# Spacing the attention groups 104 columns apart instead of 99, in the queries and keys, the scores and the masked weights

## The chip, the cores and the metric

The kernel runs on one core of one Trainium2 chip. The metric is device time in microseconds (us), the median over the executions of a run; times of a kernel on one chip scatter by about 0.3 to 1.6 us around 1248. Engines are named as in the profile: PE is the matmul engine (PEld its weight loads), DVE the vector engine, ACT the scalar engine, POOL the GpSimd engine, SP the engine that issues most loads and stores.

## The reference, cut to what matters

The reference computes two unrelated parts from two inputs of 2048 rows and joins them. Part A is a complex linear recurrence with a projection before and after it. Part B, which the change touches, is an attention over segments of 32 rows with 8 memory rows carried along:

```python
for s in range(n_seg):                       # 64 segments
    h = jnp.concatenate([mem, xs], axis=1)   # 8 memory rows + 32 rows
    q, k, v = (einsum('btd,dhe->bhte', h, W) for W in (Wq, Wk, Wv))   # 32 heads of 128
    scores = einsum('bhqe,bhke->bhqk', q, k) * scale
    p = softmax(where(mask, scores, -1e9))
    o = einsum('bhte,hed->btd', einsum('bhqk,bhke->bhqe', p, v), Wo)
    mem = o[:, :M, :]; outs.append(o[:, M:, :])
```

The kernel gathers three segments and three memory columns into a group of 99 columns; 22 groups for each head cover the input.

## The kernel before

Queries and keys of two heads (a "pair", 16 of them) lie in one tile each, group after group, 99 columns (198 bytes in bf16) apart. A score group is two groups of two heads: four score matmuls, one exponential on ACT, one product with the mask on POOL. The value matmuls take the masked product `m` as their weights. `psS` holds scores, `psO` and `psR` the values, `psP` projections.

```python
NG = 22; GX = 96; GW = 99; NU = NG // 2
QW = 2208
MW = 4 * GW + 29
...
    def att_front(self, hp, u):              # one score group
        qt, kt = self.qk[hp % 2]
        s = k.ps("S", (128, 2, 2, GW))
        for gg in range(2):
            g0 = (2 * u + gg) * GW
            for hh in range(2):
                PE.matmul(s[:, gg, hh, :], kt[:, hh, g0:g0 + 128], qt[:, hh, g0:g0 + GW], start=True, stop=True)
        e = self.p3a.tile([GW, 2, 2, GW], BF16, name="b_e", bufs=3)
        k.S.activation(e[:], s[0:GW], ACT.Exp, ...)
        m = self.mt[i % len(self.mt)]
        k.G.tensor_tensor(m[0:GW, 0:4 * GW].rearrange(...), e[:], mask..., ALU.mult)
...
    def att_back(self, blocks):              # up to three blocks of values
        for i, (_, b, m, j) in enumerate(blocks):
            PE.matmul(o[:, i, 0:EV], m[:, j * GW:j * GW + 128], vt[...], start=True, stop=True)
...
    def attention(self):
        for hp in range(HP):
            for u in range(NU):
                if u == 2:
                    self.load_v(hp + 1)
                pend += self.att_front(hp, u)
                back(8)                      # value matmuls in threes until 8 blocks are left
                yield hp, u                  # projections of the next pair fill in here
        back(0)
```

The evictions of projections into `q` and `k` are DVE copies of 480 columns, cut into five runs of 96 at the group spacing.

Of the kernel before, what the change touches and what calls it, by code (L numbers as in the profile page):

```python
# [11 lines left out]
ACT = mybir.ActivationFunctionType  # L12
# [17 lines left out]

NG = 22; GX = 96; GW = 99; NU = NG // 2
NSLOT = NG * GX
QW = 2208
NTL = 3 * NG
NMX = 7
NM = NTL + NMX
# [2 lines left out]
EV = E + 1  # L39
EW = E + 8  # L40
EO = E + 4
MW = 4 * GW + 29

XMAIN = 1920
XE = T + NM
# [291 lines left out]
class PartB:  # L337
# [223 lines left out]
    def qk_init(self, pool):  # L561
        self.qk = [[pool.tile([128, 2, QW], BF16, name=f"b_{n}{i}", bufs=1) for n in "qk"] for i in range(2)]
        self.qk_zero(0)

    def qk_zero(self, i):
        V = self.k.V
        for t in self.qk[i]:
            V.memset(t[:, :, 64 + NMX:GX], 0.0)
            V.memset(t[:, :, 21 * GW + 64:21 * GW + GX], 0.0)
            V.memset(t[:, :, NG * GW:QW], 0.0)  # L570

    def load_wqk(self, hp):
        if hp < HP:
# [6 lines left out]
    def proj(self):  # L580

        k = self.k; PE = k.PE
        for hp in range(HP):
            self.load_wqk(hp + 1)
            w = self.wqk.pop(hp)
            if hp == 1:
                self.qk_zero(1)
            NS = XE - XMAIN
            for i in range(2):
                t = self.qk[hp % 2][i]  # L590
                p = k.ps("P")
                for hh in range(2):
                    for c in range(KC):
                        PE.matmul(p[:, hh * NS:(hh + 1) * NS], w[i][:, c, hh * 128:(hh + 1) * 128], self.xe[:, c, XMAIN:XE],
                                  start=(c == 0), stop=(c == KC - 1))
                pv = p[:, 0:2 * NS].rearrange("p (h n) -> p h n", h=2)
                k.copy("v", t[:, :, 0:64], pv[:, :, 0:64])
                k.copy("v", t[:, :, 21 * GW:21 * GW + 64], pv[:, :, 64:128])
                k.copy("v", t[:, :, 64:64 + NMX], pv[:, :, 128:128 + NMX])
                k.copy("v", t[:, :, 0:NG * GW].rearrange("p h (g n) -> p h g n", n=GW)[:, :, :, GX:GW],  # L600
                       pv[:, :, 128 + NMX:NS].rearrange("p h (g j) -> p h g j", j=3))
                yield
            for q in range(4):
                for i in range(2):
                    t = self.qk[hp % 2][i]
                    for hh in range(2):
                        p = k.ps("P")
                        for c in range(KC):
                            PE.matmul(p[:, 0:480], w[i][:, c, hh * 128:(hh + 1) * 128], self.xe[:, c, 480 * q:480 * q + 480],
                                      start=(c == 0), stop=(c == KC - 1))  # L610
                        g0 = (1 + 5 * q) * GW
                        k.copy("v", t[:, hh, g0:g0 + 5 * GW].rearrange("p (g n) -> p g n", n=GW)[:, :, 0:GX],
                               p[:, 0:480].rearrange("p (g n) -> p g n", n=GX))
                        yield

# [13 lines left out]
    def att_front(self, hp, u):  # L629

        k = self.k; PE = k.PE
        qt, kt = self.qk[hp % 2]
        s = k.ps("S", (128, 2, 2, GW))
        for gg in range(2):
            g0 = (2 * u + gg) * GW
            for hh in range(2):
                PE.matmul(s[:, gg, hh, :], kt[:, hh, g0:g0 + 128], qt[:, hh, g0:g0 + GW], start=True, stop=True)
        e = self.p3a.tile([GW, 2, 2, GW], BF16, name="b_e", bufs=3)
        i = hp * NU + u
        k.S.activation(e[:], s[0:GW], ACT.Exp, scale=float(E) ** -0.5, accum_out=self.accE[0:GW, i:i + 1])  # L640
        m = self.mt[i % len(self.mt)]
        mask = k.maskA if u == 0 else k.maskB
        k.G.tensor_tensor(m[0:GW, 0:4 * GW].rearrange("p (a b q) -> p a b q", a=2, b=2), e[:],  # L643
                          mask[0:GW, :, :].unsqueeze(2).to_broadcast([GW, 2, 2, GW]), ALU.mult)
        return [(hp, 4 * u + b, m, b) for b in range(4)]

    def att_back(self, blocks):

        k = self.k; PE, V = k.PE, k.V
        hp, b0, n = blocks[0][0], blocks[0][1], len(blocks)  # L650
        vt = self.vtile[hp]
        if b0 == 0:
            self.ob = self.p3a.tile([GW, 2 * NG, E], BF16, name="b_ob", bufs=2)
        o = k.ps(("O", "O", "R")[self.nback % 3], (128, 3, EO))
        self.nback += 1
        for i, (_, b, m, j) in enumerate(blocks):
            PE.matmul(o[:, i, 0:EV], m[:, j * GW:j * GW + 128], vt[:, b // 2, (b % 2) * EW:(b % 2) * EW + EV], start=True, stop=True)
        r = self.accR[0:GW, hp * 2 * NG + b0:hp * 2 * NG + b0 + n]
        V.reciprocal(r, o[0:GW, 0:n, E])  # L659
        V.tensor_tensor(self.ob[:, b0:b0 + n, :], o[0:GW, 0:n, 0:E], r.unsqueeze(2).to_broadcast([GW, n, E]), ALU.mult)  # L660
        q, cs = hp // 4, slice((hp % 4) * 256, (hp % 4) * 256 + 256)
        on, tn = self.on[q], self.tn[q]
        ov = self.ob[:].rearrange("p (g h) e -> p g (h e)", h=2)
        early = hp == HP - 1

        def rows(g0, g1):
            r = on[64 + GX * (g0 - 1):64 + GX * (g1 - 1), :].rearrange("(g p) n -> p g n", p=GX)
            k.SP.dma_start(r[:, :, cs], ov[0:GX, g0:g1, :])
        if early and b0 + n == 2 * GE:
            rows(1, GE)  # L670
            k.SP.dma_start(on[0:64, cs], ov[0:64, 0, :])
        if b0 + n == 2 * NG:
            del self.vtile[hp]
            if early:
                rows(GE, NG - 1)
            else:
                rows(1, NG - 1)
                k.SP.dma_start(on[0:64, cs], ov[0:64, 0, :])
            k.SP.dma_start(on[T - 64:T, cs], ov[0:64, NG - 1, :])
            k.SP.dma_start(tn[0:NTL, :].rearrange("(g j) n -> j g n", j=3)[:, :, cs], ov[GX:GW, :, :])  # L680
            k.SP.dma_start(tn[NTL:NM, cs], ov[64:64 + NMX, 0, :])

    def att_init(self):
        self.vtile, self.nback = {}, 0
        self.mt = [self.p3a.tile([128, MW], BF16, name=f"b_m{i}", bufs=1) for i in range(5)]
        for m in self.mt:
            self.k.G.memset(m[:, 4 * GW:MW], 0.0)
            self.k.G.memset(m[96:128, 0:4 * GW], 0.0)
        self.load_v(0)

    def attention(self):
# [529 lines left out]
```

## Time and profile before

| | |
|---|---|
| time, median of 3 runs | 1248.03 us (1247.3 to 1248.12) |
| span of the profiled run | 1246.5 us, granted clock 0.999 |
| PE busy | 1238.4 us |
| attention stage | about 487 to 1018 us |

First, lines from the page of the kernel before: the busy time and share of each engine with its number of instructions; the busy tenths of PE and the granted clock in 40 slices of the span; and the shares of the chain of work that ended last.

```profile
span 1246.5 us, 20192 instructions
PE 1238.4 (99%) x8342; PEld 662.2 (53%) x8342; DVE 668.1 (54%) x1246; ACT 263.4 (21%) x631; POOL 276.5 (22%) x412
...
PE   9999999999999999999999999999999999999998
...
PEclk9999999999999999999999999999999999999999
...
PE 97%; DMA 2%; ACT 1%; issue 0%; POOL 0%; DVE 0%; SPq 0%; ACTq 0%
```

PE never rests, and the chain runs through it. A busy PE is not yet a PE at its peak, so the starts of successive matmuls were also subtracted from each other in the trace. Each distance is the time that one matmul occupies the stream: 216 ns for 512 columns, 202 for 480, 57 for 129, 44 to 45 for the scores' 99. The Trainium skill, page "TensorE: Matmul & The Clock Gate", section "Wait — 56ns, not 53.3ns?", gives N / 2.4 GHz plus about 2.5 ns for a warm stream. This trace agrees to within about 1 ns on average for each of these shapes (99 columns: 43.75 by that law, 44.61 measured). Everything above the law adds up to 7.0 us in the whole kernel. For the few matmuls of at most 24 columns, 25 ns was taken in place of the law, since the 128 matmuls of 4 columns start 25 ns apart here; with the bare law the sum is 10.0 us. As long as the law holds, a change that leaves the matmuls and their columns as they are cannot win more than that.

Next, the waits of PE in the kernel before: who waited for whom, total us, times, longest.

```profile
PE psR L64 <- DVE hpb L105: 1.3, 1, 1.3
PE psO L64 <- POOL b_m L643: 0.9, 3, 0.4
PE psU L64 <- DMA b_xr<-in_B_x_dram: 0.5, 1, 0.5
PE psP L64 <- ACT b_xe L89: 0.2, 1, 0.2
PE psO L64 <- issue: 0.2, 1, 0.2
```

Three of these are in the first 34 us. The three waits for `b_m` are at the end of attention; the last line is the wait before the first value matmul at 492 us.

Then the instructions that the change touches, from the views of the score tile and of the masked weights (duration in ns as min/median/max), and from the groups by form (busy us, mean ns, idle before).

```profile
L64 PE MATMUL psS<-b_q,b_k x704: 205/208/210, 487.1 to 1015.2; 128*128 128x99 bf16 x176
...
L640 ACT ACTIVATE b_e<-psS x176: 501/501/503, 487.4 to 1015.5; 99x396 bf16<-99x396 f32 x176
```

```profile
L64 PEld LDWEIGHTS <-b_m x704: 95/98/100, 492.8 to 1017.2; 128*128 128x128 bf16 x176
L64 PE MATMUL psO<-b_v,b_m x480: 217/220/231, 492.8 to 1017.1; 128*128 128x129 bf16 x160
...
L643 POOL TENSOR_TENSOR b_m<-b_e,maskB x160: 871/872/877, 489.9 to 1016.1; 99x396 bf16<-99x396 bf16 x160
```

```profile
L91 DVE CAST b_q<-psP 128x480 bf16<-128x480 f32 x128 | 84.4, 659 | 91.1 <-PE psP L64 91.1
```

A matmul's duration here (208 ns) includes its latency; the stream distance (44 ns) is what it costs when others follow. The eviction's 91.1 us of idle time before it were spent waiting for PE, so DVE follows PE and not the other way round.

### The profile page before, as it was taken

Reading aid. Unit: us, or ns where it says so; the run is one execution under the profiler, and the core shown is the slowest. Engines: PE = TensorE matmul, PEld = TensorE weight load, DVE = VectorE, ACT = ScalarE, POOL = GpSimd, SP = SyncE. Lnnn points to the kernel's source line nnn. Section 1 sums busy time; section 2 is a strip of 40 time slices with the busy share of each in tenths; the row PEclk is TensorE's granted clock in tenths of the full one; section 3 lists DMA queues with packets and bytes.
Section 4 is the critical chain, followed back from the end, with each engine's and each line's share of the span. In section 5 each row is a group of like instructions: output and inputs, shape, how many; then the busy total and the mean of one; then the engine's idle time right before and its main releaser. Section 6 shows DMA issues by size and latency. Waiting matters only on the chain.

```text
span 1246.5 us, 20192 instructions
## 1 busy us (share of the span) xinstructions
PE 1238.4 (99%) x8342; PEld 662.2 (53%) x8342; DVE 668.1 (54%) x1246; ACT 263.4 (21%) x631; POOL 276.5 (22%) x412
## 2 busy tenths in 40 slices
PE   9999999999999999999999999999999999999998
PEld 4444444444455555656666656555665554446444
DVE  4688899998711124666666666666666641001000
ACT  5344444443310000211111111111211110000000
POOL 4111331212322321322222222222222220000000
PEclk9999999999999999999999999999999999999999
DMA  9975444554898734665454544545473279407000
GB/s 236 267 205 150 130 131 128 144 156 108 240 322 248 250 116 94 182 176 122 96 144 108 144 108 113 138 91 133 97 155 95 60 222 225 107 18 153 17 17 27
DMA packets 316023, 176.83 MB, mean 142 GB/s; under 512 B 138651, under 2 KB 301327, under 8 KB 315927
## 3 DMA queue, kind: packets, MB, share of 16 engines
q1 hardware_dynamic: 293830, 147.95, 48.4%
q10 hardware_dynamic: 21072, 24.38, 5.8%
q0 software_dynamic: 1024, 3.17, 0.7%
q8 instruction: 66, 1.08, 0.4%
q14 instruction: 31, 0.25, 0.1%
HBM read 89.14 MB, written 53.17 MB: 114 GB/s over the span
## 4 chain that ended last, share of the span: by engine, by line
PE 97%; DMA 2%; ACT 1%; issue 0%; POOL 0%; DVE 0%; SPq 0%; ACTq 0%
PE psP L64 81%; PE psU L64 9%; PE psS L64 3%; PE psO L64 2%; PE psR L64 2%; DMA wo<-in_B_Wo_dram 1%; DMA b_vx<-b_vst 1%; DMA b_xr<-in_B_x_dram 0%; ACT b_vst L89 0%; ACT L187 0%; ACT b_xe L89 0%; POOL b_m L643 0%; ACT a_fr L236 0%; ACT a_k L233 0%; ACT a_k L229 0%
## 5 line engine op out<-in xcount | busy, mean ns | idle before, releaser
L64 PE MATMUL psP<-b_xe,b_wq 128*128 128x480 bf16 (+1 forms) x1280 | 247.7, 343 | 0.0
L64 PE MATMUL psP<-b_xe,b_wk 128*128 128x480 bf16 (+1 forms) x1280 | 247.7, 343 | 0.0
L64 PE MATMUL psP<-b_wv,b_xe 128*128 128x512 bf16 (+2 forms) x1048 | 224.6, 372 | 0.3 <-ACT b_xe L89 0.2
L643 POOL TENSOR_TENSOR b_m<-b_e,maskB 99x396 bf16<-99x396 bf16 x160 | 139.6, 872 | 334.8 <-ACT b_e L640 334.8
L640 ACT ACTIVATE b_e<-psS 99x396 bf16<-99x396 f32 x176 | 88.2, 501 | 532.8 <-PE psS L64 528.5
L64 PEld LDWEIGHTS <-b_wk 128*128 128x128 bf16 x1280 | 119.4, 98 | 94.2
L64 PEld LDWEIGHTS <-b_xe 128*128 128x128 bf16 x1056 | 101.9, 98 | 119.4 <-issue 0.6
L64 PEld LDWEIGHTS <-b_wq 128*128 128x128 bf16 x1280 | 118.7, 98 | 87.7
L91 DVE CAST b_k<-psP 128x480 bf16<-128x480 f32 (+1 forms) x192 | 98.2, 533 | 100.9 <-PE psP L64 100.9
L91 DVE CAST b_q<-psP 128x480 bf16<-128x480 f32 (+1 forms) x192 | 98.2, 533 | 93.1 <-PE psP L64 91.5
L64 PEld LDWEIGHTS <-b_ol 128*128 128x128 bf16 x864 | 84.3, 98 | 94.4
L64 PE MATMUL psU<-a_xT,a_bt 128*128 128x512 bf16 x512 | 114.9, 379 | 0.0
L64 PE MATMUL psP<-t,a_hl 128*128 128x512 bf16 x512 | 113.1, 379 | 0.0
L91 DVE CAST b_ost<-psP 128x512 bf16<-128x512 f32 (+1 forms) x17 | 11.5, 676 | 183.4 <-PE psP L64 183.4
L64 PE MATMUL psP<-wo,b_ol 128*128 128x512 bf16 (+1 forms) x448 | 92.5, 364 | 0.0
L64 PE MATMUL psP<-t,b_ol 128*128 128x512 bf16 x416 | 92.2, 379 | 0.0
L280 POOL TENSOR_SCALAR a_tt<-a_pr,a_tabf 128x1 f32<-128x1 f32 x48 | 34.1, 710 | 243.5 <-DVE a_pr L275 243.5
L660 DVE TENSOR_TENSOR b_ob<-psO,b_accR 99x384 bf16<-99x384 f32 x160 | 85.9, 553 | 2.5 <-DVE b_accR L659 0.3
L89 ACT ACTIVATE b_vst<-psP 128x512 bf16<-128x512 f32 x126 | 72.1, 589 | 71.4 <-PE psP L64 60.3
L267 DVE TENSOR_TENSOR a_pr<-psU,a_tabf 128x2048 f32<-128x2048 f32 x32 | 73.0, 2283 | 14.8 <-PE psU L64 14.7
L64 PEld LDWEIGHTS <-a_bt 128*128 128x128 bf16 x512 | 49.2, 98 | 57.6
L64 PEld LDWEIGHTS <-a_hl 128*128 128x128 bf16 x512 | 49.0, 98 | 56.7
(199 smaller groups left out, 964.2 us busy)
## 6 DMA issues: line engine op xcount, KB each, us to landing
b_v<-b_vx SPq DMA_DIRECT2D x16, 1122.0 KB
b_wv<-in_B_Wv_dram SPq DMA_DIRECT2D x16, 1024.0 KB
b_on<-b_ob SPq DMA_DIRECT2D x15, 960.0 KB
b_vx<-b_vst ACTq DMA_DIRECT2D x24, 544.0 KB
a_hs<-a_h SPq DMA_DIRECT2D x32, 256.0 KB
b_wog<-in_B_Wo_dram SPq DMA_DIRECT2D x4, 2048.0 KB
b_wq<-in_B_Wq_dram SPq DMA_DIRECT2D x16, 512.0 KB
b_wk<-in_B_Wk_dram SPq DMA_DIRECT2D x16, 512.0 KB
```

Source lines behind the costliest of these rows:

```text
L64: r = f(*a, **kw)
L89: self.S.activation(out, in_, ACT.Copy)
L91: self.V.tensor_copy(out, in_)
L267: V.tensor_tensor(pr[:], u[:].unsqueeze(1).to_broadcast([128, 2, 2, TB]), view(t3, [[TB + 1, 2], [TB + 1, 2], [1, TB]]), ALU.mult)
L280: G.tensor_scalar(tt[:, j:j + 1], w[:, j, TB - 1:TB], t3[:, 1, TB:TB + 1], None, ALU.mult)
L640: k.S.activation(e[:], s[0:GW], ACT.Exp, scale=float(E) ** -0.5, accum_out=self.accE[0:GW, i:i + 1])
L643: k.G.tensor_tensor(m[0:GW, 0:4 * GW].rearrange("p (a b q) -> p a b q", a=2, b=2), e[:], mask[0:GW, :, :].unsqueeze(2).to_broadcast([GW, 2 ...
L660: V.tensor_tensor(self.ob[:, b0:b0 + n, :], o[0:GW, 0:n, 0:E], r.unsqueeze(2).to_broadcast([GW, n, E]), ALU.mult)
```

## The change

Groups start every 104 columns, 208 bytes, which is a multiple of 16. The matmuls keep their 99 columns; the gap is zeroed once. The intent is to give each operand an aligned start. The core of the diff (the same replacement of `GW` by `GP` in the evictions is cut):

```diff
-QW = 2208
+GP = 104; QW = NG * GP + 24
-MW = 4 * GW + 29
+MW = 4 * GP + 24
...
+            V.memset(t[:, :, 0:NG * GP].rearrange("p h (g n) -> p h g n", n=GP)[:, :, :, GW:GP], 0.0)
...
-        s = k.ps("S", (128, 2, 2, GW))
+        s = k.ps("S", (128, 2, 2, GP))
-            g0 = (2 * u + gg) * GW
+            g0 = (2 * u + gg) * GP
-                PE.matmul(s[:, gg, hh, :], kt[:, hh, g0:g0 + 128], qt[:, hh, g0:g0 + GW], start=True, stop=True)
+                PE.matmul(s[:, gg, hh, 0:GW], kt[:, hh, g0:g0 + 128], qt[:, hh, g0:g0 + GW], start=True, stop=True)
-        k.S.activation(e[:], s[0:GW], ACT.Exp, ...)
+        k.S.activation(e[:], s[0:GW, :, :, 0:GW], ACT.Exp, ...)
-        k.G.tensor_tensor(m[0:GW, 0:4 * GW].rearrange("p (a b q) -> p a b q", a=2, b=2), e[:],
+        k.G.tensor_tensor(m[0:GW, 0:4 * GP].rearrange("p (a b q) -> p a b q", a=2, b=2)[:, :, :, 0:GW], e[:],
...
-            PE.matmul(o[:, i, 0:EV], m[:, j * GW:j * GW + 128], ...
+            PE.matmul(o[:, i, 0:EV], m[:, j * GP:j * GP + 128], ...
...
-            self.k.G.memset(m[:, 4 * GW:MW], 0.0)
-            self.k.G.memset(m[96:128, 0:4 * GW], 0.0)
+            self.k.G.memset(m[:], 0.0)
```

More of the change, by code (lines that the diff above doesn't have):

```diff
@@ L568, in qk_zero @@
             V.memset(t[:, :, 64 + NMX:GX], 0.0)
-            V.memset(t[:, :, 21 * GW + 64:21 * GW + GX], 0.0)
-            V.memset(t[:, :, NG * GW:QW], 0.0)
+            V.memset(t[:, :, 21 * GP + 64:21 * GP + GX], 0.0)
+            V.memset(t[:, :, 0:NG * GP].rearrange("p h (g n) -> p h g n", n=GP)[:, :, :, GW:GP], 0.0)
+            V.memset(t[:, :, NG * GP:QW], 0.0)
     def load_wqk(self, hp):
@@ L597, in proj @@
                 k.copy("v", t[:, :, 0:64], pv[:, :, 0:64])
-                k.copy("v", t[:, :, 21 * GW:21 * GW + 64], pv[:, :, 64:128])
+                k.copy("v", t[:, :, 21 * GP:21 * GP + 64], pv[:, :, 64:128])
                 k.copy("v", t[:, :, 64:64 + NMX], pv[:, :, 128:128 + NMX])
-                k.copy("v", t[:, :, 0:NG * GW].rearrange("p h (g n) -> p h g n", n=GW)[:, :, :, GX:GW],
+                k.copy("v", t[:, :, 0:NG * GP].rearrange("p h (g n) -> p h g n", n=GP)[:, :, :, GX:GW],
                        pv[:, :, 128 + NMX:NS].rearrange("p h (g j) -> p h g j", j=3))
@@ L610, in proj @@
                                       start=(c == 0), stop=(c == KC - 1))
-                        g0 = (1 + 5 * q) * GW
-                        k.copy("v", t[:, hh, g0:g0 + 5 * GW].rearrange("p (g n) -> p g n", n=GW)[:, :, 0:GX],
+                        g0 = (1 + 5 * q) * GP
+                        k.copy("v", t[:, hh, g0:g0 + 5 * GP].rearrange("p (g n) -> p g n", n=GP)[:, :, 0:GX],
                                p[:, 0:480].rearrange("p (g n) -> p g n", n=GX))
@@ L632, in att_front @@
         qt, kt = self.qk[hp % 2]
-        s = k.ps("S", (128, 2, 2, GW))
+        s = k.ps("S", (128, 2, 2, GP))
         for gg in range(2):
-            g0 = (2 * u + gg) * GW
+            g0 = (2 * u + gg) * GP
             for hh in range(2):
-                PE.matmul(s[:, gg, hh, :], kt[:, hh, g0:g0 + 128], qt[:, hh, g0:g0 + GW], start=True, stop=True)
+                PE.matmul(s[:, gg, hh, 0:GW], kt[:, hh, g0:g0 + 128], qt[:, hh, g0:g0 + GW], start=True, stop=True)
         e = self.p3a.tile([GW, 2, 2, GW], BF16, name="b_e", bufs=3)
         i = hp * NU + u
-        k.S.activation(e[:], s[0:GW], ACT.Exp, scale=float(E) ** -0.5, accum_out=self.accE[0:GW, i:i + 1])
+        k.S.activation(e[:], s[0:GW, :, :, 0:GW], ACT.Exp, scale=float(E) ** -0.5, accum_out=self.accE[0:GW, i:i + 1])
         m = self.mt[i % len(self.mt)]
         mask = k.maskA if u == 0 else k.maskB
-        k.G.tensor_tensor(m[0:GW, 0:4 * GW].rearrange("p (a b q) -> p a b q", a=2, b=2), e[:],
+        k.G.tensor_tensor(m[0:GW, 0:4 * GP].rearrange("p (a b q) -> p a b q", a=2, b=2)[:, :, :, 0:GW], e[:],
                           mask[0:GW, :, :].unsqueeze(2).to_broadcast([GW, 2, 2, GW]), ALU.mult)
@@ L656, in att_back @@
         for i, (_, b, m, j) in enumerate(blocks):
-            PE.matmul(o[:, i, 0:EV], m[:, j * GW:j * GW + 128], vt[:, b // 2, (b % 2) * EW:(b % 2) * EW + EV], start=True, stop=True)
+            PE.matmul(o[:, i, 0:EV], m[:, j * GP:j * GP + 128], vt[:, b // 2, (b % 2) * EW:(b % 2) * EW + EV], start=True, stop=True)
         r = self.accR[0:GW, hp * 2 * NG + b0:hp * 2 * NG + b0 + n]
```

## The prediction

> **What bounds the kernel now.** TensorE: busy 1238.4 of 1246.5 us on the profile's page, at a granted clock of 0.999; the chain of waits is 97% PE. From the trace I took the distances between successive matmul starts: 216 ns for 512 columns, 202 for 480, 57 for 129, 44 to 45 for 99. The Trainium skill, page "TensorE: Matmul & The Clock Gate", section "Wait — 56ns, not 53.3ns?", states N / 2.4 GHz plus about 2.5 ns for a warm stream; this trace agrees within 1 ns. Summed over all 8342 matmuls, everything above that law is 7.0 us: about 4.1 us in the first 34 us, 1.8 us of four waits for masked weights (at 492 us and in the last 10 us of attention), 0.3 us near 1158 us, and some 0.6 us spread over the score matmuls. The change does not alter the number of matmuls or columns.
>
> **What the change does.** Spacing 99 columns (198 bytes) becomes 104 (208 bytes, a multiple of 16). Built side by side, PE's and ACT's instruction order is identical; DVE gets four more memsets, POOL loses five, and one K-weight load is queued behind two output stores, long before it is needed.
>
> - Score matmuls (704). Their excess depends on the group's place modulo 8, as a 16-byte effect would: most last 43.3 to 44.2 ns, some 45, and the last ones of groups 2 and 5 modulo 8 take 47.5 and 47.3. The skill's page "SBUF — State Buffer", "Specifications", gives 16-byte lines with a penalty for crossings; the trace shows at most 3.5 ns, on 95 matmuls. If all become like group 0 (44.15 ns), the sum saved is 0.3 us (estimate): the only gain on the critical path.
> - Attention-value matmuls: their weights start at 198-byte steps today, yet all four positions take 56.5 to 56.8 ns; weight loads take 98 ns everywhere, hidden. Gain 0.
> - Evictions of Q and K on DVE: 657 to 662 ns at every offset; the 64-column copies 283 ns at one place, 291 at the other. DVE is 63% busy in the attention stage and PE never waits for these. Gain 0.
> - ACT's exponential (501 ns) and POOL's mask product (872 ns) get four rows of 99 in place of one run of 396. I expect a change under 5%, either way. PE waits for POOL only four times; 40 ns each would be 0.2 us.
> - Added memsets of 220 elements: 0.2 to 0.3 us each, estimated from the 64-element ones (110 ns). Two stand before the first Q and K evictions at 472 us, where DVE idles 0.35 us; the rest goes into the three projection buffers and does not reach PE.
>
> **Prediction.** 1247.7 us, range 1246.2 to 1249.2 (8 in 10), set mostly by run-to-run spread (1247.3 to 1248.1 before). Faster by over 2%: 1%; within 2%: 98%; slower by over 2%: 1%.
>
> **What shows each step right or wrong.** Right: score distances uniform near 44 ns, those of 47 gone; value matmuls still 57; Q and K evictions within 3 ns of 659; the same four PE waits. Wrong: weight loads not 98 ns; PE waits on psS, psP or masked weights between 500 and 1000 us; POOL's product over 1 us.
>
> **What would make it wrong.** If POOL slowed beyond about 2.6 us per product (the spacing of score groups), masked weights would stall PE throughout. If the memsets or the later K-weight load held up projections, PE would show one new gap. A gain of 2% is out of reach with 7 us above the streaming law.

## The result, and the profile after

| | before | after |
|---|---|---|
| first comparison, medians (4 runs each) | 1247.91 us | 1247.37 us |
| ratio, 95% interval | | 0.9997 (0.9979 to 1.0014) |
| second comparison, medians (9 and 5 runs) | 1247.74 us | 1247.68 us |
| ratio, 95% interval | | 1.0000 (0.9987 to 1.0014) |

A ratio is the mean time of one kernel's fast runs over that of the other's in the same rounds, so it is not quite the ratio of the medians quoted. All profiled runs compared here granted a clock of 0.999 or 1.0; single runs have an unknown state, and only their distances inside the trace are used.

Lines from the page of the kernel after, as above:

```profile
span 1245.6 us, 20120 instructions
PE 1234.4 (99%) x8270; PEld 662.3 (53%) x8342; DVE 668.0 (54%) x1250; ACT 263.5 (21%) x631; POOL 275.8 (22%) x407
...
PE   9999999999999999999999999999999999999998
...
PEclk9999999999999999999999999999999999999999
...
PE 98%; DMA 1%; issue 0%; ACT 0%; POOL 0%; DVE 0%; SPq 0%; ACTq 0%
```

PE's busy time looks 4.0 us lower, but this is no gain: the line counts 8270 matmuls against 8342 weight loads, so 72 matmul records are missing from this trace. A second profile of the kernel before also has 8270. The score and value matmuls (704 each) are complete in both.

The waits of PE after:

```profile
PE psR L64 <- DVE hpb L105: 1.3, 1, 1.3
PE psO L64 <- POOL b_m L644: 0.9, 3, 0.4
PE psP L64 <- ACT b_xe L89: 0.2, 1, 0.2
```

The touched instructions after, from the same three views, with an added memset:

```profile
L64 PE MATMUL psS<-b_q,b_k x704: 207/208/208, 486.8 to 1014.3; 128*128 128x99 bf16 x176
...
L641 ACT ACTIVATE b_e<-psS x176: 501/501/503, 487.2 to 1014.6; 99x396 bf16<-99x396 f32 x176
```

```profile
L64 PEld LDWEIGHTS <-b_m x704: 95/98/99, 492.2 to 1016.4; 128*128 128x128 bf16 x176
L64 PE MATMUL psO<-b_v,b_m x480: 220/220/231, 492.2 to 1016.3; 128*128 128x129 bf16 x160
...
L644 POOL TENSOR_TENSOR b_m<-b_e,maskB x160: 872/874/877, 489.7 to 1015.3; 99x396 bf16<-99x396 bf16 x160
```

```profile
L91 DVE CAST b_q<-psP 128x480 bf16<-128x480 f32 x128 | 84.2, 658 | 91.4 <-PE psP L64 91.4
...
L570 DVE MEMSET b_q<- 128x220 bf16 x2 | 0.5, 242 | 0.0
```

Only the narrower spread of the scores (207 to 208 ns, 205 to 210 before) and of the value matmuls into `psO` (from 220 ns, 217 before) betrays the change. The profiled spans differ by 0.855 us, and four marks on PE split that difference:

| stretch of PE's time | before, us | after, us | difference |
|---|---|---|---|
| span's start to first score matmul | 487.066 | 486.838 | -0.228 |
| first score to first value matmul | 5.770 | 5.390 | -0.380 |
| first value matmul to last score matmul | 522.327 | 522.112 | -0.215 |
| last score matmul to the end | 231.302 | 231.270 | -0.032 |

The question for the experiments is which of these belong to the change.

The second row is visible in the timeline of PE around the first value matmul (start us, duration, what, idle time before it). Before:

```profile
492.28 0.34 PE L64 MATMUL psS<-b_q,b_k 128*128 128x99 bf16 x4
492.84 0.50 PE L64 MATMUL psO<-b_v,b_m 128*128 128x129 bf16 x6 [0.21 <-issue]
```

After:

```profile
492.05 0.34 PE L64 MATMUL psS<-b_q,b_k 128*128 128x99 bf16 x4
492.23 0.50 PE L64 MATMUL psO<-b_v,b_m 128*128 128x129 bf16 x6
```

Before, the first value matmul starts 0.56 us after the four scores begin; after, 0.18 us, with no wait.

### The profile page after: what moved, and what is told of

It reads as the page before. It is cut to its first block, busy times and chain, and to the rows that moved or that the text cites. A ratio compares the mean times of both kernels' runs of the same rounds, so it can differ in the third digit from the quotient of the medians.

```text
span 1245.6 us, 20120 instructions
## 1 busy us (share of the span) xinstructions
PE 1234.4 (99%) x8270; PEld 662.3 (53%) x8342; DVE 668.0 (54%) x1250; ACT 263.5 (21%) x631; POOL 275.8 (22%) x407
## 4 chain that ended last, share of the span: by engine, by line
PE 98%; DMA 1%; issue 0%; ACT 0%; POOL 0%; DVE 0%; SPq 0%; ACTq 0%
PE psP L64 82%; PE psU L64 9%; PE psS L64 3%; PE psO L64 2%; PE psR L64 2%; DMA wo<-in_B_Wo_dram 1%; DMA b_xr<-in_B_x_dram 0%; ACT b_xe L89 0%; POOL b_m L644 0%; DVE b_ost L91 0%; SPq L64 0%; ACT b_e L641 0%; ACTq L89 0%
```

## The experiments

Theory: of the difference, only some 0.2 to 0.3 us in the attention stage belongs to the change, because queries start on a line of SBUF; the rest is when loads happen to land. Rivals: the spacing of the scores in PSUM or of the weights does it; the wait at 492 us is removed by the change; the difference is noise as a whole; PE or POOL has slack or limits that the streaming law hides.

### Both kernels again, and each half of the change alone

No edit for the first two. The third takes the change for queries and keys only, the fourth for scores and masked weights only:

```diff
 # qk104_only, against the changed kernel
-        s = k.ps("S", (128, 2, 2, GP))
+        s = k.ps("S", (128, 2, 2, GW))
 # and m at j * GW, MW = 4 * GW + 29

 # sm104_only, against the kernel before
-        s = k.ps("S", (128, 2, 2, GW))
+        s = k.ps("S", (128, 2, 2, GP))
 # and m at j * GP, MW = 4 * GP + 24; q and k stay at GW
```

> The kernel before, unchanged, as a second look. My theory (the small steps near 5 to 45 us and the wait before the first value matmul at 492 us come from when loads land, not from the change): the pattern of the score matmuls repeats within 0.3 ns (47.5 and 47.3 ns for the last of groups 2 and 5 modulo 8, 45 in groups 1 and 7), and the wait at 492 us differs from 0.38 us by 0.1 us or more. Rival (that wait belongs to the 99-column layout): 0.38 us again. Time 1247.3 to 1248.3 us, ratio 1.000.

> The changed kernel, unchanged, timed in the same rounds. My theory: ratio to before 0.9995 to 0.9999 (0.1 to 0.6 us), of which about 0.3 us are the score matmuls, all at 44.1 to 44.3 ns. Rival (the difference seen first was noise as a whole): ratio 1.000 and no sign. The wait at 492 us may come or not; the rival that the change removes it says none.

> Only the queries and keys lie every 104 columns; scores in PSUM and masked weights stay at 99. My theory (the score gain comes from where the operands start in SBUF): all score matmuls 44.1 to 44.3 ns, sum of the excess over the streaming law down from 0.6 to 0.3 us; evictions of Q and K 658 ns; value matmuls 56.6 as before; POOL's product 872 ns as before. Rival (spacing of the scores in PSUM): the 47 ns distances stay.

> Only the scores in PSUM and the masked weights lie every 104 columns; queries and keys stay at 99. My theory: the 47.5 and 47.3 ns distances stay, excess of the score matmuls 0.6 us; POOL's product 874 ns; weight loads 98 ns. Rival (spacing in PSUM): all at 44.2 ns.

Measured on one chip, 5 rounds; distances are means from the trace, without those in which PE waited:

| kernel | median us | ratio (95%) | score distance, ns | value distance, ns | first value to last score, us | gap before first value, us |
|---|---|---|---|---|---|---|
| before (first look) | | | 44.61 | 56.60 | 522.327 | 0.42 |
| before, again | 1247.76 | 1.0000 (0.9986 to 1.0014) | 44.61 | 56.60 | 522.325 | 0.62 |
| after (first look) | | | 44.17 | 56.72 | 522.112 | 0.04 |
| after, again | 1247.68 | 1.0000 (0.9987 to 1.0014) | 44.16 | 56.70 | 522.109 | 0.58 |
| queries and keys only | 1247.40 | 0.9997 (0.9983 to 1.0011) | 44.16 | 56.71 | 522.106 | 0.24 |
| scores and masked weights only | 1247.87 | 1.0000 (0.9987 to 1.0014) | 44.61 | 56.75 | 522.439 | 0.39 |

The last column is the distance from the start of the last score matmul before the first value matmul to that value matmul; 0.044 us of it are the score matmul itself.

What follows. The stretch from the first value matmul to the last score repeats within 3 ns for a kernel, so its 0.215 us are the change's (two looks at each of the two kernels), and the queries and keys alone give all of it. The score matmuls fall from 44.61 to 44.17 ns, 704 x 0.44 = 0.31 us; the value matmuls rise by 0.11 ns, 704 x 0.11 = 0.08 us, and the two nearly make the sum. The scores' spacing in PSUM gives nothing: with it alone the pattern of 47.5 and 47.3 ns stays. Why the value matmuls cost 0.1 ns more in every variant of this table, even with the masked weights left at 99 (where 56.6 ns was expected), is open; in the kernels with shifted queries below they range from 56.5 to 56.8 ns.

The gap before the first value matmul belongs to no layout: 0.42 and 0.62 us before, 0.04 and 0.58 us after. It follows the load of V. The last packet of the first V load ends at 491.65 us in the first look at the kernel before and at 490.88 after. In nine of the ten profiled runs with this schedule and single POOL and score instructions, the first weight load on `m` starts 1.14 to 1.18 us after that last packet; in the tenth, the first look at the kernel after, it came 1.31 us after it, and PE found the load already landed. The masked weights of the first six blocks were ready at least 1.6 us earlier in all ten. So the second row of the split is the landing of a load. The first row isn't the change either: the 0.23 us are already there at 67 us (the same matmul starts at 67.27 us before and 67.04 after), long before the first instruction that the change touches, a memset at 459 us, and the two looks at the kernel before differ by 0.63 us at this mark. Together the two rows are 0.61 of the 0.855 us. The repeat of the changed kernel came out only 0.06 us under before, a ratio of 1.0000 where 0.9995 to 0.9999 was expected.

### Where in a line the operands start

The changed kernel, with the query or key tile moved by a few columns; each kernel tests two shifts, one for even and one for odd pairs of heads.

```diff
-        self.qk = [[pool.tile([128, 2, QW], BF16, name=f"b_{n}{i}", bufs=1) for n in "qk"] for i in range(2)]
+        sh = {"q": (5, 6), "k": (0, 0)}      # columns of 2 bytes
+        self.qk = [[pool.tile([128, 2, QW + 8], BF16, name=f"b_{n}{i}", bufs=1)[:, :, sh[n][i]:sh[n][i] + QW] for n in "qk"] for i in range(2)]
```

> The changed kernel with every query group moved off the 16-byte boundary: by 10 bytes for even pairs of heads (99 columns then end exactly with the 13th line of 16 bytes) and by 12 bytes for odd pairs (they need a 14th line). My theory, number of 16-byte lines that the moving operand touches: even pairs unchanged near 44.2 ns, odd pairs show distances of about 47.5 ns in at least one of each two score matmuls, which adds 0.5 to 1.1 us over the 352 matmuls of the odd pairs. Rival 1, the key side (weights) costs it: no change anywhere. Rival 2, it costs only where two neighbouring groups start at different places in a line: no change anywhere, as all groups of a pair start alike.

> The changed kernel with every key group moved by 2 bytes for even pairs of heads and by 12 bytes for odd pairs; queries stay on the boundary. My theory: score matmuls 44.1 to 44.3 ns in both, weight loads 98 ns. Rival (the weights' start costs the 3 ns): odd pairs near 47.5 ns.

> Queries 2 bytes off the boundary in even pairs of heads (13 lines of 16 bytes), 14 bytes off in odd pairs (14 lines). The 10-byte shift cost 0.65 ns a matmul where the pure count of lines said nothing, the 12-byte shift 1.73 ns. Theory now: a start anywhere inside a line costs about 0.65 ns, a 14th line 1.1 more: means 44.8 and 45.9 ns. Rival (cost grows evenly with the offset): about 44.3 and 46.1 ns.

> Queries 6 bytes off the boundary in even pairs, 8 bytes in odd pairs, both within 13 lines. Theory (any start inside a line costs about 0.65 ns): 44.8 ns in both. Rival (cost grows evenly with the offset, 1.73 ns at 12 bytes): 45.0 and 45.3 ns. Pure count of lines: 44.2 in both.

Mean distance of the score matmuls, one look each. Starts are counted from the start of the tile, which is taken to lie on a 16-byte line; the trace doesn't show addresses.

| start of the query group, bytes past a multiple of 16 | lines of 16 bytes touched by 198 bytes | mean distance, ns |
|---|---|---|
| 0 (changed kernel) | 13 | 44.17 |
| 2 | 13 | 44.81 |
| 6 | 13 | 44.79 |
| 8 | 13 | 44.17 |
| 10 | 13 | 44.82 |
| 12 | 14 | 45.90 |
| 14 | 14 | 45.99 |

Keys moved by 2 and by 12 bytes: 44.17 ns both, weight loads 97.9 ns. So the weights' start costs nothing at these two places, and the rival on the key side falls, as does the one that only a change of offset between neighbours costs: here all groups of a pair start alike. The moving operand's start does cost. A 14th line costs 1.7 to 1.8 ns, at just the two starts where the count of lines puts one. But 10 bytes cost 0.65 ns where I expected nothing, and after I had changed the theory to "any start inside a line costs 0.65", 8 bytes cost nothing. Neither theory fits all rows. The rows of this table fit a rule with two terms, starts at 2, 6 and 10 bytes (no multiple of 4) costing 0.6 ns and a 14th line costing 1.7 to 1.8; 4 bytes alone was not tried. But the rule does not carry over to the kernel before, where neighbouring groups start at different places. With 4 bytes taken as free it gives a mean of 44.9 ns there, against 44.61 measured: groups at 2 bytes, each right after one at 12, take 43.4 ns; groups at 12 and 14 bytes show the 47 ns in the second head alone (44.2 and 43.9 in the first); and group 12, at 8 bytes, shows 46.5 ns in its first head. So what one start costs depends on the matmuls around it, and a single distance can hold a neighbour's cost. The mechanism stays open. A bound on its size does not: the worst start everywhere would cost 704 x 1.82 = 1.3 us (an estimate from the last row), 0.1% of the kernel.

### Is PE bound by its stream?

```diff
-                PE.matmul(s[:, gg, hh, 0:GW], kt...
+                for _ in range(2):
+                    PE.matmul(s[:, gg, hh, 0:GW], kt...
```

> The changed kernel with each of the 704 score matmuls issued twice (the second overwrites the first, so the result is the same). My theory (the kernel is bound by the column stream of TensorE alone): 704 x 44.2 ns = 31.1 us longer, 1278.5 us, within 1 us. Rival (PE has hidden slack, so small changes of a matmul's length are absorbed by waits): clearly less than 31 us.

Measured: correct, 1278.77 us against 1247.50 of before in the same rounds, ratio 1.0246 (1.0229 to 1.0264). The 31.3 us are the expected 31.1 within the scatter, and the 1408 score matmuls keep 44.17 ns. The columns added to PE's stream here are paid in full.

### POOL's slack

```diff
+        for _ in range(2):
-        k.G.tensor_tensor(m[0:GW, 0:4 * GP]...
+            k.G.tensor_tensor(m[0:GW, 0:4 * GP]...
```

> The changed kernel with POOL's mask product issued twice per score group, so POOL spends 1.75 us per group in place of 0.87. My theory (POOL has slack up to the spacing of the groups, 2.6 us): nothing between 495 and 1000 us; only the three or four waits at the end of attention grow, by 0.9 us each at most, so 1.5 to 3.5 us in all and 1249 to 1251 us. Rival (POOL paces the score groups): 176 x 0.87 = 153 us longer, or at least tens of us.

Measured: correct, 1281.19 us against 1247.50, ratio 1.0269 (1.0252 to 1.0286): 33.7 us, far from the 1.5 to 3.5 expected. The waits of PE show it at once:

```profile
PE psO L64 <- POOL b_m L645: 20.0, 34, 1.2
PE psR L64 <- POOL b_m L645: 6.3, 15, 0.4
```

My theory took POOL's slack from a spacing of the groups of 2.6 us, as if they were even. (In the trace the mean is 3.0 us.) The timelines say what the slack really is. After the change, with one product:

```profile
534.49 0.34 PE L64 MATMUL psS<-b_q,b_k 128*128 128x99 bf16 x4
...
535.60 0.87 POOL L644 TENSOR_TENSOR b_m<-b_e,maskB 99x396 bf16<-99x396 bf16 x1 [2.71 <-ACT b_e L641]
...
536.39 0.34 PE L64 MATMUL psS<-b_q,b_k 128*128 128x99 bf16 x4
...
536.57 0.33 PE L64 MATMUL psO<-b_v,b_m 128*128 128x129 bf16 x3
```

With two products (the same place, 2.1 us later in this longer run):

```profile
536.61 0.34 PE L64 MATMUL psS<-b_q,b_k 128*128 128x99 bf16 x4
...
537.73 3.73 POOL L645 TENSOR_TENSOR b_m<-b_e,maskB 99x396 bf16<-99x396 bf16 x4 [1.76 <-ACT b_e L641]
...
538.51 0.34 PE L64 MATMUL psS<-b_q,b_k 128*128 128x99 bf16 x4
...
538.69 0.28 PE L64 MATMUL psO<-b_v,b_m 128*128 128x129 bf16 x2
...
539.61 0.23 PE L64 MATMUL psO<-b_v,b_m 128*128 128x129 bf16 x1 [0.65 <-POOL b_m L645]
```

Groups are not evenly spaced: 1.9 us here, 3.6 us in many other places. And value matmuls go in threes while four blocks come at a time, so some threes reach into the group whose scores were issued just one step before. There the product ends at 535.60 + 0.87 = 536.47 us, and PE wants it at 536.6. Taken over the trace of the changed kernel, the time from the end of a product to the first weight load on it is 0.15 to 0.16 us for 15 groups and about 0.39 us for some 31 more, and less only for a few at the end of attention. Making each product 0.92 us later and adding up what exceeds these margins gives 32.0 us of waits, an estimate close to the 33.7 measured. It is rough: the second products really end 0.95 us after the first, and a load that waited starts some 0.05 us after its product, so that much of each margin is no slack; with both the sum is 36.3 us.

### One group more between scores and values

This tests that explanation, and the claim that what is left above the streaming law is waits. It holds back twelve blocks; the next load of V, the first output projections and the load that belongs to them move one group later, and one filler stands before the last values.

```diff
-                if u == 2:
+                if u == 3:
                     self.load_v(hp + 1)
-                back(8)
+                back(12)
                 yield hp, u
+        yield HP, 0
         back(0)
...
-            if done == 18 * HP:
+            if done == 18 * HP and n >= 170:
```

> The changed kernel with value matmuls one score group later (twelve blocks held back, not eight), the next V load and the early load of the last head pair one group later with them, and one filler of four output-projection matmuls before the last value matmuls. My theory (what is left above the streaming law in the attention stage is waits of value matmuls for their operands, not alignment): the wait at 492 us (0.04 to 0.6 us so far) and the three at the end of attention (0.36, 0.42, 0.60 us) go, score matmuls stay at 44.2 ns; 1.0 to 1.9 us less than the changed kernel, 1245.6 to 1246.6 us. Rival (those waits only move elsewhere): 1247.2 to 1247.7 us.

> The same, with POOL's mask product issued twice. The doubled product cost 33.7 us where my theory said 1.5 to 3.5, so the theory of POOL's slack (mean spacing of the groups) has fallen. New theory: value matmuls that take 6 blocks at once reach into the group whose scores were issued only one step before; in the changed kernel's trace the masked weights are then ready only 0.155 us (15 groups) or 0.39 us (32 groups) before their first weight load, and making each 0.92 us later gives 32.0 us of waits. One group more of distance adds at least 1.9 us of slack: the 33 us go, apart from at most 4 us at the end of attention where groups are 1.2 us apart; 1246 to 1250.5 us. Rival (POOL's throughput, or its sharing of SBUF with DVE, costs the 33 us): still 1270 us or more.

Measured on one chip: before 1247.70 us; with twelve blocks 1245.94 us, ratio 0.9985 (0.9972 to 0.9999); with twelve blocks and the doubled product 1248.66 us, ratio 1.0007 (0.9992 to 1.0022). Both are correct. The waits of PE with twelve blocks, where no wait for `b_m` is left:

```profile
PE psR L64 <- DVE hpb L105: 1.3, 1, 1.3
PE psU L64 <- DMA b_xr<-in_B_x_dram: 0.3, 1, 0.3
PE psP L64 <- ACT b_xe L89: 0.2, 1, 0.2
```

With twelve blocks and the doubled product:

```profile
PE psO L64 <- POOL b_m L645: 2.4, 3, 1.2
PE psR L64 <- DVE hpb L105: 1.3, 1, 1.3
```

The 33.7 us shrink to 2.7 (1248.66 - 1245.94), all at the end of attention where groups are 1.2 us apart. So POOL's throughput, and anything that its doubled work may take from other engines, are not what cost; the distance between a product and its use is. The twelve-block version is the fastest of all here, by 1.8 us on before, which is still within 2%.

## Why the prediction was right

- **The time.** 1247.7 us was forecast and 1247.37 and 1247.68 were measured. The forecast rested on one argument: PE streams all the time and its column count does not change. The doubled scores confirm it, 31.3 us for 31.1. The time alone proves little: the range was 3 us wide, and a forecast gain of 0.3 us is within the scatter of the runs. That the first medians lay 0.54 us apart in the right direction was luck; in the repeat it was 0.06.
- **The score matmuls.** Forecast 0.3 us, measured 0.31 us on the scores alone, of which 0.08 us went back into value matmuls for a reason that stays open. The forecast tied it to 16-byte lines. The groups with the 47 ns matmuls, 2 and 5 modulo 8, are those that touch a 14th line, and the shifts show that a 14th line costs time; but the smaller cost of other starts, and how it falls on neighbours, is not explained by lines.
- **Value matmuls, weight loads, evictions, ACT, POOL.** Forecast no change beyond a few per cent: value matmuls +0.1 ns, weight loads 98 ns, evictions 659 to 658 ns, exponential 501 and 501, product 872 to 874. Keys moved by 2 and 12 bytes cost nothing.
- **The memsets and the later K-weight load.** 242 ns per memset, as estimated; the waits of PE show no new line for them.
- **Wrong in a detail: "1.8 us of four waits for masked weights (at 492 us ...)".** The one at 492 us follows the load of V, by a nearly constant 1.14 to 1.18 us after its last packet in nine runs, while the masked weights had long been ready. It moved the first comparison by more than the change did. The same sentence's "about 4.1 us in the first 34 us" comes out as 3.5 us when it is added up again from the trace.
- **Wrong: "If POOL slowed beyond about 2.6 us per product (the spacing of score groups), masked weights would stall PE throughout".** The step that failed is taking the slack of a stage from an even spacing of its work. At 1.8 us a product already costs 33.7 us; the tightest of the repeated margins is 0.15 us. The change made the product 1.5 ns longer, so this error did not touch the result; that was luck in so far as a product 20% longer (0.17 us, an estimate) would already be past that margin.

## What to carry to other kernels

Before aligning anything, add up what lies above the streaming law on the bounding engine; here that sum was 7 us of 1247, so no spacing of the same columns could matter, and the waits in it were worth more than the alignment. A difference of 0.07% between two profiles must be split at fixed marks and repeated: the part that came back within 3 ns was the change; the rest changed from run to run. And an engine's slack is the margin between its result and the first use at the tightest place, read from the trace one by one; 22% busy and a mean spacing did not show it here.

## What the Trainium skill lacked or had wrong

- "SBUF — State Buffer", section "Specifications", names 16-byte lines and a penalty for crossings, but gives no size for a matmul's moving operand. Here 99 bf16 columns take 44.17 ns when they start at 0 or 8 bytes past a line, 44.8 at 2, 6 or 10, and 45.9 to 46.0 at 12 or 14, when all groups start alike. The pages used do not name the cost of starts at 2, 6 and 10 bytes.
- "TensorE: Matmul & The Clock Gate": nothing there says that the weights' start matters or not. Keys moved by 2 and by 12 bytes changed neither the weight loads (97.9 ns) nor the matmuls (44.17 ns).
- The same page, section "Back-to-back issue gap", gives about 81 ns a matmul for 128 columns and about 131 ns for 512 in a stream of weight loads and matmuls. This kernel is such a stream, with 8342 weight loads for 8342 matmuls, and shows 57 ns for 129 columns and 216 ns for 512: the page's N / 2.4 plus 2.5 ns, which it calls isolated, is what holds here.
- "DMA: Bandwidth & Descriptors", section "Anatomy of one DMA — SWDGE (gpsimd) path", gives a fixed cost of about 2 us for a DMA on GpSimd's path, most of it the confirmation after the last byte, without a number of its own for the part after the last packet, and not for loads issued by SP. Here, for a load issued by SP, the first weight load that waited for V started 1.14 to 1.18 us after the load's last packet, in nine runs.
